# A Strassen product over two token blocks in the last layer-1 stage of an attention and maxout kernel

## The chip, the cores and the metric

The kernel runs on one core of one Trainium2 chip. The metric is the device time of one execution, in microseconds (us). TensorE does the matmuls, VectorE, ScalarE and GpSimd the elementwise work, and SyncE issues the transfers. In the profile these engines are called PE (PEld is its weight load), DVE, ACT, POOL and SP.

## The reference, cut to what matters

There are 8 batches, 8 heads, 576 positions of 64 numbers. The attention output of every token is the sum of two attentions: one over keys and values averaged four by four, repeated four times, and one over the local window of seven positions. Then every token's 512 numbers go through a maxout layer and an output layer:

```
h = np.maximum(np.maximum(x @ w1, x @ w2), x @ w3)    # x 4608 x 512, w 512 x 768
return (h @ w_out).astype(np.float32)                 # w_out 768 x 512
```

## The kernel before

Tokens are cut into blocks of 512. Block j (0 to 7) holds the first 512 tokens of batch j, and block 8 the last 64 tokens of each of the eight batches ("the tail block"). B is 8, so blocks B-1 and B are the last two.

For each block the attention is computed in two halves of four heads (`scores`, `pooled_scores`, `values`, `pooled_values`; n = 2j and 2j+1). The local window runs on VectorE, ScalarE and GpSimd: products `prod` and a reduction for the scores, then seven products per head into `pv` and a reduction over them into `x`. `transposes` turns `x` by TensorE, adds the pooled attention (`od`, `odtail`), and splits the result into a rounded part `xhi` and a remainder `xlo`. The weights are split in the same way into `whi` and `wlo` and stay in SBUF. A product of two split matrices is made of three matmuls: high by high, low by high, high by low.

`mlp_in(j)` is layer 1. For each of six groups of 128 hidden units (ft) and each of the three weight matrices (i) it does 4 chunks of 128 inputs times 3 matmuls, 12 in all, on 512 tokens, into one PSUM bank; the maximum over i is taken by VectorE, and the result is split into `hh`. One block takes 6 x 3 x 12 = 216 matmuls. `mlp_out(j)` is layer 2: 4 groups of 18 matmuls, a copy by ScalarE and a store.

All work is first recorded (`Recorder.add`) with a priority, and then `place` orders it: it goes through time with a cost for each operation, gives each engine the ready operation with the smallest start, priority and number, picks an engine where several may do an operation (`tt` allows VectorE and GpSimd), and hands out the buffers of each tag in the order of recording. The result is a fixed order on each engine. In that plan an operation of VectorE with two SBUF sources and any operation of GpSimd exclude one another (`port`). All instructions are issued in `emit`, so that the trace names line 390 for nearly all of them; tiles tell them apart. PSUM has four banks `pm`, three `pa` and one `pq`.

The main loop records `mlp_in(j)`, `mlp_out(j)`, then `turn(j + 1)` (the transposes of the next block) and `block(j + 2)` (the attention two blocks on). The high and low parts of x have one buffer each, so the parts of one block are made when layer 1 of the block before has ended.

Of the kernel before, what the change touches and what calls it, by code (L numbers as in the profile page):

```python
# [41 lines left out]
SETS = (5, 4, 3, 2, 5, 4, 5, 5)  # L42
STAGE = ("hh0", "hh1", "hh2", "hh3", "hh4", "hh5", "wo3", "wo4", "wo5", "hh3", "hh4", "hh5", "pv", "pv", "pv", "pv", "hh5", "pv")
STAGE_OUT = ("hh5", "hh4", "hh5", "hh4", "pv", "pv")
WO_ORDER = (2, 3, 4, 5, 0, 1)
F64_LO = float(np.array(0x38000000, np.uint32).view(np.float32))
F64_HI = float(np.array(0x47EFFFFF, np.uint32).view(np.float32))
# [40 lines left out]
class Recorder:  # L88
# [264 lines left out]
    def emit(self):  # L353
        out = self.place()
        store, words = {}, {}
        for tag, (bufs, infos) in self.tags.items():
            words[tag] = max(i["words"] for i in infos)

        def home(space, tag, i, kind):
            slot = (space, tag, i, kind)  # L360
            if slot not in store:
                name = f"{tag}_{i}"
                store[slot] = self.pools[space].tile([128, words[space, tag]], kind, tag=name, name=name + ("r" if kind == F32R else ""))
            return store[slot]

        def real(a):
            info = self.of.get(a.tensor.name) if is_ap(a) else None
            if info is None:
                return a
            (space, tag), width = info["tag"], words[info["tag"]]  # L370
            kind = F32R if info["dtype"] == F32R else F32
            base = home(space, tag, info["slot"], kind)
            dims = [list(d) for d in a.ap]
            p0, f0 = divmod(a.offset, dims[0][0])
            if a.dtype == BF16:
                base, width = base.bitcast(BF16), 2 * width
            dims[0][0] = width
            r = bass.AP(tensor=base.tensor, offset=base.offset + p0 * width + f0, ap=dims)
            return r if a.dtype in (kind, BF16) else r.bitcast(a.dtype)

        self.pools["SB"].tile([128, 8], F32, tag="pad", name="pad")
        for space, tag in self.tags:
            if tag.startswith(("whi", "wlo", "hh", "wo", "xhi", "xlo")) and tag != "hqk":
# [18 lines left out]
def local_global_attention_maxout_kernel(ctx: ExitStack, tc: tile.TileContext, q, k, v, w1, w2, w3, w_out, ident_d, mask_d, band_d, out):  # L402
# [285 lines left out]
    def values(n):  # L688
        j, h0 = n // 2, HH * (n % 2)
        st = state[n]  # L690
        p = st["p"]
        blk = state["blk", j]
        if j < B:
            hv = new([P, HH, 2 * D], tag="hv", name=f"hv_{n}")
            vd = st["vd"] = new([P, HH, D], tag="vd", bufs=2, name=f"vd_{n}")
        for g in range(HH):
            h = h0 + g
            if g % 2 == 0:
                x = blk["x"][h // 2] = new([P, FAC, 2, D], tag="x", bufs=XBUFS, name=f"x_{j}_{h // 2}")
# [186 lines left out]
    def mlp_out(j):  # L886
        h, wo = state["blk", j]["h"], state["wo"]
        for f in range(FAC):
# [10 lines left out]
                dst = dram(out, (FAC * P + f) * DM, [[S * DM, B], [FAC * DM, TAIL], [1, DM]])  # L899
            sp.dma_start(dst, y)  # L900

    def attention(n):
        j = n // 2
        if n % 2 == 0:
# [76 lines left out]


# [24 lines left out]
```

## Time and profile before

| what | value |
|---|---|
| time, median of 3 runs | 794.75 us (793.41 to 794.94) |
| time of the profiled execution | 794.03 us |
| its span in the trace | 792.3 us |
| TensorE busy | 751.6 us, 95% |
| VectorE busy | 623.9 us, 79% |
| ScalarE busy | 416.9 us, 53% |
| GpSimd busy | 311.4 us, 39% |

The span runs from the first to the last instruction of the trace; the time of the execution is 1.7 us longer. A matmul's recorded length is longer than the distance to the next one, since matmuls overlap in the array, so the price of one is read from a run of many.

### The profile page before, as it was taken

The numbers are of one execution on the slowest core, as the hardware profiler recorded it, in microseconds if no ns is written. First come the engines' busy times: TensorE is split into PE (matmuls) and PEld (weight loads), VectorE is DVE, ScalarE is ACT, GpSimd is POOL, SyncE is SP. The second block draws the span as 40 slices with busy tenths as digits, with TensorE's granted clock in tenths as the row PEclk, the third lists the DMA queues.
The fourth block names the chain that finished last, engine by engine and source line by source line (L and its number), as shares of the span: only waits on it lengthen the run. The fifth ranks groups of instructions, "written<-read, shape, count | busy, mean of one in ns | idle before, by whom it ended". The sixth has DMA issues, their size and how long they took to land. (4 is left out here: it accounts for less than half of the span.)

```text
span 792.3 us, 12159 instructions
## 1 busy us (share of the span) xinstructions
PE 751.6 (95%) x3992; PEld 593.9 (75%) x3992; DVE 623.9 (79%) x910; ACT 416.9 (53%) x1437; POOL 311.4 (39%) x555
## 2 busy tenths in 40 slices
PE   3889999999999999999999999899999999999997
PEld 2667777778787778677777887678777878888885
DVE  3889997998998999999999999899989765231220
ACT  2766676635755846577285545656583543121111
POOL 0000200225749738597584646657272423000000
PEclk9655999999999999999999999999999999999999
DMA  7985234315334334344254333433341211001002
GB/s 166 234 278 155 63 107 121 120 41 172 106 103 159 111 89 127 104 151 135 70 158 121 111 90 105 142 96 118 89 154 48 84 40 47 1 14 40 1 1 53
DMA packets 74293, 81.77 MB, mean 103 GB/s; under 512 B 29656, under 2 KB 54550, under 8 KB 74230
## 3 DMA queue, kind: packets, MB, share of 16 engines
q1 hardware_dynamic: 74230, 81.00, 34.3%
q8 instruction: 31, 0.51, 0.3%
q14 instruction: 32, 0.26, 0.1%
HBM read 71.54 MB, written 9.44 MB: 102 GB/s over the span
## 5 line engine op out<-in xcount | busy, mean ns | idle before, releaser
L390 PE MATMUL pm<-xhi_0r,wlo_0r 128*128 128x512 f32 x648 | 256.5, 396 | 0.3 <-DVE wlo_0r L390 0.3
L390 PE MATMUL pm<-xhi_0r,whi_0r 128*128 128x512 f32 x648 | 256.7, 396 | 0.0
L390 PE MATMUL pm<-xlo_0r,whi_0r 128*128 128x512 f32 x648 | 255.6, 395 | 0.0
L390 POOL TENSOR_TENSOR pv<-v,s 128x256 f32<-128x256 f32 x262 | 155.4, 698 | 83.8 <-DVE s L390 69.9
L390 PE MATMUL pm<-wo_0r,hh_0r 128*128 128x512 f32 x648 | 156.2, 394 | 1.3 <-DVE hh_0r L390 0.8
L390 PEld LDWEIGHTS pm<-xhi_0r,wlo_0r 128*128 128x128 f32 x648 | 122.5, 189 | 26.1 <-DVE wlo_0r L390 0.7
L390 PEld LDWEIGHTS pm<-xhi_0r,whi_0r 128*128 128x128 f32 x648 | 122.5, 189 | 25.8 <-issue 1.0
L390 PEld LDWEIGHTS pm<-xlo_0r,whi_0r 128*128 128x128 f32 x648 | 122.4, 189 | 25.5 <-issue 1.1
L390 ACT ACTIVATE pv<-v,s 128x64 f32<-128x64 f32 x520 | 136.4, 412 | 9.3 <-DMA v<-in_v_dram 4.8
L390 PEld LDWEIGHTS pm<-wo_0r,hh_0r 128*128 128x128 f32 x648 | 120.0, 188 | 27.6 <-DVE hh_0r L390 1.4
L390 DVE TENSOR_TENSOR prod<-k,pq 128x1792 f32<-128x1792 f32 x56 | 112.8, 2015 | 8.4 <-DMA k<-in_k_dram 5.5
L390 DVE TENSOR_REDUCE pq<-prod 128x28 f32<-128x1792 f32 x56 | 113.2, 2022 | 2.2 <-ACT pq L390 1.3
L390 DVE TENSOR_REDUCE x<-pv 128x256 f32<-128x1792 f32 x48 | 96.0, 2012 | 7.4 <-ACT pv L390 4.4
L390 ACT CAST hh_0r<-pm 128x512 fp32r<-128x512 f32 x54 | 31.8, 588 | 95.2 <-DVE pm L390 95.2
L390 DVE TENSOR_TENSOR t<-pm,t 128x512 f32<-128x512 f32 x54 | 37.0, 685 | 54.6 <-PE pm L390 54.1
L390 POOL TENSOR_TENSOR th<-traw 128x128 f32<-128x128 f32 x38 | 18.2, 480 | 128.8 <-DVE vs L390 74.2
L390 ACT COPY pq<-q 128x256 f32<-128x256 f32 x56 | 21.5, 384 | 67.1 <-DVE pq L390 37.6
L390 DVE TENSOR_TENSOR pm<-pm,t 128x512 f32<-128x512 f32 x54 | 37.4, 693 | 22.3 <-PE pm L390 21.9
L390 ACT COPY y<-pm 128x512 f32<-128x512 f32 x41 | 23.9, 590 | 49.9 <-PE pm L390 39.6
L390 ACT COPY t<-pm 128x512 f32<-128x512 f32 x54 | 31.8, 589 | 32.6 <-PE pm L390 32.4
L390 DVE TENSOR_TENSOR hh_0r<-pm,hh_0r 128x512 fp32r<-128x512 f32 x54 | 36.9, 684 | 9.8 <-ACT hh_0r L390 9.4
L390 POOL TENSOR_TENSOR hqk<-k 128x128 f32<-128x128 f32 x48 | 22.2, 464 | 29.2 <-DMA k<-in_k_dram 28.6
(160 smaller groups left out, 891.8 us busy)
## 6 DMA issues: line engine op xcount, KB each, us to landing
k<-in_k_dram SPq DMA_DIRECT2D x55, 320.0 KB
v<-in_v_dram SPq DMA_DIRECT2D x55, 320.0 KB
out_dram<-y SPq DMA_DIRECT2D x36, 256.0 KB
q<-in_q_dram SPq DMA_DIRECT2D x56, 128.0 KB
hh<-in_moe_w_dram SPq DMA_DIRECT2D x10, 512.0 KB
pv<-in_moe_w_dram SPq DMA_DIRECT2D x5, 512.0 KB
traw<-in_q_dram SPq DMA_DIRECT2D x16, 128.0 KB
v<-in_v_dram SPq DMA_DIRECT2D x16, 128.0 KB
```

The source lines that it names most:

```text
L390: getattr(self.engines[o.eng], method)(*map(real, args), **{k: real(x) for k, x in kw.items()})
```

## The change

Layer 1 of blocks 7 and 8 is no longer done block by block. For a pair of hidden groups (fa, fb) and one weight matrix (a step; there are nine) the product is a 2 by 2 block matrix product: the weights are cut by hidden group (fa, fb) and by input half (chunks 0 and 1, chunks 2 and 3), the tokens by block (7, 8) and by input half. Strassen's form (Winograd's variant) does it with 7 block products in place of 8. A block product is 2 chunks x 3 matmuls = 6 matmuls, so a step has 42 instead of 48. The four sums of weights are made per step by `combos` and split by `parts`; the sums of tokens are made once by `pair_operands`. The results are put together by additions behind the matmuls in `joint_in`. Layer 2 of both blocks follows. For the second half of the tail block's attention (n = 17) the `v` tiles of its last two heads take buffers of `k`, and VectorE may take the `pv` products too. The rest of the diff gives a buffer a new tile each time that its type changes.

```diff
-            vv = new([P, HW], tag="v", bufs=2, name=f"v_{n}_{g}")
+            vv = new([P, HW], tag="k" if n > 2 * B and g > 1 else "v", bufs=2, name=f"v_{n}_{g}")
...
-                rec.add({"ACT": muls, "POOL": [("tensor_tensor", (), kw)]})
+                one = [("tensor_tensor", (), kw)]
+                rec.spare = 0.0 if n > 2 * B else rec.spare
+                rec.add({"ACT": muls, "POOL": one, "DVE": one} if n > 2 * B else {"ACT": muls, "POOL": one})
...
+    def split(pair, src):
+        act.copy(pair[0], src)
+        tt(pair[1], src, pair[0].bitcast(F32), ALU.subtract)
+
+    def pair_operands():
...
+        state["sums"] = {0: combos(0)}
+        state["parts"] = {0: parts(0, state["sums"][0])}
+        prod, qkT, pvs = room("prod", 1, 3), room("qkT", 2, 1, wide) + room("qkT", 2, 1, wide), room("pv", 2, 3) + room("pv", 2, 3)
+        b22 = [tuple(room("k", 2) + room("hqk", 2)), tuple(room("k", 2) + room("pd"))]
...
+        for c in range(NCC):
...
+            for f in range(FAC):
+                pe.transpose(ps[:, f], x[:, f], ident)
...
+            dve.tensor_tensor(out=xc.rearrange("p (f r) -> p f r", f=FAC), in0=ps, in1=od, op=ALU.add)
+            if c < 2:
+                f = new([P, FAC * P], tag="od", bufs=2, name=f"t1_{c}")
+                f1.append(f)
+                tt(f, xc, blk["hi"][c].bitcast(F32), ALU.subtract)
+                tt(f, f, blk["lo"][c].bitcast(F32), ALU.subtract)
+                split(t1[c], f)
+        state["sums"][1] = combos(1)
+        state["parts"][1] = parts(1, state["sums"][1])
+        state["sums"][2] = combos(2)
+        rec.prio = -150.0
+        for c in range(2):
+            f, d, y = f1[c], xs[c], xs[c + 2]
+            tt(f, y, f, ALU.subtract)
+            split(t2[c], f)
+            tt(d, y, d, ALU.subtract)
+            split(t3[c], d)
+            split(b22[c], y)
...
+            tt(f, blk["hi"][c + 2].bitcast(F32), f, ALU.subtract)
+            tt(f, f, blk["lo"][c + 2].bitcast(F32), ALU.add)
+            split(t4[c], f)
...
+    def combos(step):
+        engines = ("DVE", "POOL") if step < 2 else ("POOL",)
...
+            f = [new([P, 2, 2 * P], tag=tag, bufs=bufs, name=f"f{x}_{step}") for x, (tag, bufs) in enumerate(homes)]
+        for x, ft in ((0, fa), (1, fb)):
+            flat = [w[ft][:, i].rearrange("p c t -> p (c t)").bitcast(F32) for w in (whi, wlo)]
+            tt(f[x].rearrange("p a t -> p (a t)"), *flat, ALU.add, engines)
+        (a11, a12), (a21, a22), (s1, s2), (s3, s4) = [(t[:, 0], t[:, 1]) for t in f]
+        tt(s1, a21, a22, ALU.add, engines)
+        tt(s2, s1, a11, ALU.subtract, engines)
+        tt(s3, a11, a21, ALU.subtract, engines)
+        tt(s4, a12, s2, ALU.subtract, engines)
...
+    def joint_in(xt):
...
+        def first(step):
...
+            product(ps, plain[:2], xt[1], True)
+            act.copy(p1, ps)
+            product(ps, plain[2:], xt[2], False)
+            if i == 0:
...
+                act.copy(low[ft], ps)
+            else:
+                dve.tensor_tensor(out=low[ft] if i == 1 else ps, in0=ps, in1=low[ft], op=ALU.max)
...
+        def second(step, t):
...
+            product(pd, w[1], xt[5], True)
+            act.copy(p5, pd)
...
+        for step in range(4):
+            early[step] = first(step)
+        for step in range(2):
+            early[step] += second(step, early[step][1])
+        for step in range(9):
...
+            if 0 < step < 8:
+                f = state["sums"].get(step + 1) or combos(step + 1)
+                state["parts"][step + 1] = parts(step + 1, f)
+            p1, t = early[step][:2] if step in early else first(step)
+            pd, w, p5 = early[step][2:] if step < 2 else second(step, t)
...
+            p6 = new([P, 4 * P], tag="x", bufs=XBUFS, name=f"p6_{step}")
+            product(pb, w[2], xt[6], True)
+            act.copy(p6, pb)
+            product(pb, w[3], xt[7], False)
+            dve.tensor_tensor(out=p5, in0=pb, in1=p5, op=ALU.add)
+            tt(p6, p1, p6, ALU.add)
+            product(pd, w[4], xt[3], False)
+            product(pb, w[7], xt[4], False)
...
+            tt(out[2], p5, p1, ALU.add)
+            dve.tensor_tensor(out=out[0], in0=pd, in1=p6, op=ALU.add)
+            dve.tensor_tensor(out=out[1], in0=pb, in1=p1, op=ALU.add)
+            if i > 0:
+                for r, src, engines in zip(run, out, (("DVE",), ("DVE",), ("DVE", "POOL"))):
+                    tt(r if i == 1 else src, src, r, ALU.max, engines)
...
-    for j in range(B + 1):
+    for j in range(B - 1):
         with at(-100.0):
             mlp_in(j)
             mlp_out(j)
-        if j < B:
-            turn(j + 1)
-        if j < B - 1:
-            block(j + 2)
+        turn(j + 1)
+        block(j + 2)
+    with at(100.0 * 2 * (B + 1)):
+        xt = pair_operands()
+    with at(-100.0):
+        joint_in(xt)
+        mlp_out(B - 1)
+        mlp_out(B)
```

`parts(step, f)`, not shown, splits the four sums of a step: in odd steps two casts and two subtractions of 128 x 512, in even steps four casts, three subtractions of 128 x 256 and two of 128 x 128. `finish`, not shown, is the cast and the subtraction that split a finished hidden group. `product` issues the 6 matmuls.

## Rows read from the trace of the kernel before

**Rows 1.** The page, its parts 1 and 2: busy time of each engine in the whole span, and the granted TensorE clock in forty equal slices (a digit is tenths of full speed).

```profile
PE 751.6 (95%) x3992; PEld 593.9 (75%) x3992; DVE 623.9 (79%) x910; ACT 416.9 (53%) x1437; POOL 311.4 (39%) x555
...
PEclk9655999999999999999999999999999999999999
```

**Rows 2.** The busy time of each engine in stretches of the second half (columns: stretch, then busy us and count for PE, weight load, VectorE, ScalarE, GpSimd; then granted clock, DMA share, GB/s).

```profile
620.00:640.00 20.00, 18.16 (x86) 14.72 (x86) 15.39 (x18) 7.52 (x21) 7.23 (x9) 1.00 0.16 48
640.00:657.70 17.70, 17.70 (x81) 14.45 (x80) 10.20 (x14) 10.09 (x34) 7.41 (x13) 1.00 0.28 87
657.70:704.50 46.80, 46.80 (x209) 38.67 (x208) 17.38 (x22) 10.32 (x22) 3.87 (x7) 1.00 0.01 5
704.50:786.60 82.10, 82.08 (x364) 67.65 (x362) 15.52 (x23) 12.23 (x21) 0.00 (x0) 1.00 0.08 23
```

**Rows 3.** The chain that ended last, from 637 us to the end (columns: start us, length us, what).

```profile
638.93 18.37 PE pm L390 x80
...
657.74 46.75 PE pm L390 x206
...
704.93 81.67 PE pm L390 x360
...
786.66 0.59 ACT y L390
```

**Rows 4.** VectorE in order of time near the end of the kernel, around layer 2 of the last full block and after it.

```profile
702.88 2.05 DVE L390 TENSOR_TENSOR xlo_0r<-pa,xhi_0r 128x512 fp32r<-128x512 f32 x3 [0.31 <-ACT xhi_0r L390]
...
726.85 0.69 DVE L390 TENSOR_TENSOR t<-pm,t 128x512 f32<-128x512 f32 x1 [18.64 <-PE pm L390]
729.50 0.70 DVE L390 TENSOR_TENSOR pm<-pm,t 128x512 f32<-128x512 f32 x1 [1.96 <-PE pm L390]
730.85 0.69 DVE L390 TENSOR_TENSOR hh_0r<-pm,hh_0r 128x512 fp32r<-128x512 f32 x1 [0.65 <-ACT hh_0r L390]
```

**Rows 5.** Groups of one operation and shape, GpSimd over the whole span (columns: instruction, count, busy us, mean ns of one, idle before).

```profile
L390 POOL TENSOR_TENSOR pv<-pv 128x512 f32<-128x512 f32 x8 | 10.0, 1252 | 0.6
...
L390 POOL TENSOR_TENSOR qd<-hqk 128x256 f32<-128x256 f32 x12 | 8.9, 740 | 7.0 <-PE pa L390 6.9
...
L390 POOL TENSOR_TENSOR th<-pd 128x128 f32<-128x128 f32 x1 | 0.5, 454 | 15.3 <-DMA pd<-in_k_dram 15.3
```

**Rows 6.** The same kind of groups for VectorE between 40 and 200 us.

```profile
L390 DVE TENSOR_TENSOR wlo_0r<-hqk,whi_0r 128x512 fp32r<-128x512 f32 x16 | 11.0, 686 | 1.6 <-ACT whi_0r L390 1.5
...
L390 DVE TENSOR_TENSOR t<-pm,t 128x512 f32<-128x512 f32 x8 | 5.5, 685 | 1.0 <-PE pm L390 1.0
...
L390 DVE TENSOR_TENSOR vd<-hv 128x256 f32<-128x256 f32 x3 | 1.3, 418 | 0.0
```

**Rows 7.** The same kind of groups for ScalarE between 40 and 200 us: casts that read SBUF, casts that read PSUM, and quarters of a local-window product.

```profile
L390 ACT CAST whi_0r<-hqk 128x512 fp32r<-128x512 f32 x17 | 10.6, 626 | 4.2 <-DVE hqk L390 4.2
...
L390 ACT CAST hh_0r<-pm 128x512 fp32r<-128x512 f32 x7 | 4.1, 588 | 5.6 <-DVE pm L390 5.6
...
L390 ACT ACTIVATE pv<-v,s 128x64 f32<-128x64 f32 x16 | 4.0, 409 | 0.0
```

**Rows 8.** VectorE in order of time from 80 us, where two-source SBUF operations follow one another.

```profile
80.63 0.68 DVE L390 TENSOR_TENSOR wlo_0r<-hqk,whi_0r 128x512 fp32r<-128x512 f32 x1
81.23 1.29 DVE L390 TENSOR_TENSOR xlo_0r<-t,xhi_0r 128x512 fp32r<-128x512 f32 x2
...
83.90 0.68 DVE L390 TENSOR_TENSOR q<-whi 128x256 f32<-128x256 f32 x1
```

**Rows 9.** GpSimd in order of time, the stretch of Rows 8.

```profile
80.62 2.54 POOL L390 TENSOR_TENSOR th<-pt 128x128 f32<-128x128 f32 x1 [22.21 <-PE pa L390]
83.24 0.58 POOL L390 TENSOR_TENSOR vs<-th 128x64 f32<-128x64 f32 x1
```

**Rows 10.** VectorE in order of time, the last attention (the chunk of tail tokens) and what follows (columns: start us, length us, instruction, and in brackets the idle time before it and what ended it).

```profile
642.40 2.02 DVE L390 TENSOR_REDUCE pq<-prod 128x28 f32<-128x1792 f32 x1
...
646.28 0.27 DVE L390 TENSOR_TENSOR s<-pq,z 128x112 f32<-128x112 f32 x1
650.54 2.02 DVE L390 TENSOR_REDUCE x<-pv 128x256 f32<-128x1792 f32 x1 [3.99 <-ACT pv L390]
...
654.00 2.02 DVE L390 TENSOR_REDUCE x<-pv 128x256 f32<-128x1792 f32 x1
...
658.61 2.02 DVE L390 TENSOR_REDUCE x<-pv 128x256 f32<-128x1792 f32 x1
...
661.98 2.02 DVE L390 TENSOR_REDUCE x<-pv 128x256 f32<-128x1792 f32 x1 [0.21 <-POOL pv L390]
```

**Rows 11.** GpSimd in order of time, the stretch of Rows 10.

```profile
646.63 5.28 POOL L390 TENSOR_TENSOR pv<-v,s 128x256 f32<-128x256 f32 x9 [18.78 <-DVE s L390]
655.58 3.01 POOL L390 TENSOR_TENSOR pv<-v,s 128x256 f32<-128x256 f32 x5 [3.66 <-DMA v<-in_v_dram]
658.96 2.98 POOL L390 TENSOR_TENSOR pv<-v,s 128x256 f32<-128x256 f32 x5 [0.38 <-DMA v<-in_v_dram]
```

**Rows 12.** TensorE in order of time: idle gaps before single groups of matmuls.

```profile
601.18 1.09 PE L390 MATMUL pa<-ident,x 128*128 128x128 f32 x8 [1.23 <-ACT odtail L390]
...
637.00 1.25 PE L390 MATMUL pa<-ident,x 128*128 128x128 f32 x8 [1.84 <-DVE xlo_0r L390]
```

More of the change, by code (lines that the diff above doesn't have):

```diff
@@ L44 @@
 STAGE_OUT = ("hh5", "hh4", "hh5", "hh4", "pv", "pv")
+ALIGNED = ("prod", "pv", "hqk", "hv", "pd", "pt", "qkT", "k", "v", "q", "qd", "kd", "traw", "vd", "tq", "th")
+H_LAST = ("whi0", "wlo0", "whi2", "wlo2", "whi3", "wlo3")
 WO_ORDER = (2, 3, 4, 5, 0, 1)
@@ L357, in emit, with home @@
             words[tag] = max(i["words"] for i in infos)
-        def home(space, tag, i, kind):
-            slot = (space, tag, i, kind)
+            last, turns = {}, {}
+            for i in infos:
+                kind = i["dtype"] == F32R
+                if last.get(i["slot"]) != kind:
+                    last[i["slot"]] = kind
+                    turns[i["slot"], kind] = turns.get((i["slot"], kind), -1) + 1
+                i["turn"] = turns[i["slot"], kind]
+        def home(space, tag, i, kind, turn=0):
+            slot = (space, tag, i, kind, turn)
             if slot not in store:
                 name = f"{tag}_{i}"
-                store[slot] = self.pools[space].tile([128, words[space, tag]], kind, tag=name, name=name + ("r" if kind == F32R else ""))
+                store[slot] = self.pools[space].tile([128, words[space, tag]], kind, tag=name, name=name + ("r" if kind == F32R else "") + (f"t{turn}" if turn else ""))
             return store[slot]
@@ L371, in real @@
             kind = F32R if info["dtype"] == F32R else F32
-            base = home(space, tag, info["slot"], kind)
+            base = home(space, tag, info["slot"], kind, info["turn"])
             dims = [list(d) for d in a.ap]
@@ L382, in emit @@
         for space, tag in self.tags:
-            if tag.startswith(("whi", "wlo", "hh", "wo", "xhi", "xlo")) and tag != "hqk":
+            if tag.startswith(("whi", "wlo", "hh", "wo", "xhi", "xlo")) or tag in ALIGNED:
                 for i in range(self.tags[space, tag][0]):
@@ new lines, in combos @@
+    def combos(step):
+        engines = ("DVE", "POOL") if step < 2 else ("POOL",)
+        fa, fb, i = 2 * (step // 3), 2 * (step // 3) + 1, step % 3
+        if step == 1:
+            f = [new([P, 2, 2, 2 * P], tag=tag, name=f"f_{tag}_{step}") for tag in ("hh0", "hh1")]
+            f = [t[:, x] for t in f for x in range(2)]
+        else:
+            homes = [("hv", 1), ("pd", 1), ("qkT", 2), ("qkT", 2)] if step == 0 else [("x", XBUFS)] * 4
+            f = [new([P, 2, 2 * P], tag=tag, bufs=bufs, name=f"f{x}_{step}") for x, (tag, bufs) in enumerate(homes)]
[7 more added lines that the diff above has]
+        tt(s4, a12, s2, ALU.subtract, engines)
+        return f
@@ new lines, in parts @@
+    def parts(step, f):
+        fb, i = 2 * (step // 3) + 1, step % 3
+        (a11, a12), (a21, a22), (s1, s2), (s3, s4) = [(t[:, 0], t[:, 1]) for t in f]
+        s = {}
+        if step % 2 == 0:
+            homes = [("q", 2), ("q", 2), ("vd", 2), ("vd", 2), ("qd", 1), ("kd", 1), ("traw", 1)]
+            t = [new([P, 2 * P], F32R, tag=tag, bufs=bufs, name=f"sum{x}_{step}") for x, (tag, bufs) in enumerate(homes)]
+            halfs = [[u[:, c * P : c * P + P] for c in range(2)] for u in t]
+            halfs.append([new([P, P], F32R, tag=tag, name=f"sum_{tag}_{step}") for tag in ("tq", "th")])
+            for x, m, src in ((0, 2, s2), (1, 1, s1), (2, 3, s3), (3, 4, s4)):
+                s[m] = list(zip(*halfs[2 * x : 2 * x + 2]))
+                if m != 4:
+                    split(t[2 * x : 2 * x + 2], src)
+                    continue
+                act.copy(t[6], src)
+                for c, (hi, lo) in enumerate(s[m]):
+                    tt(lo, src[:, c * P : c * P + P], hi.bitcast(F32), ALU.subtract)
+        else:
+            tags = ("hh2", "hh3") if step < 4 else ("whi1", "wlo1")
+            hi, lo = [new([P, 2, 4 * P], F32R, tag=tag, name=f"s_{tag}_{step}") for tag in tags]
+            for x in range(2):
+                split((hi[:, x], lo[:, x]), f[2 + x].rearrange("p a t -> p (a t)"))
+            for m in range(1, 5):
+                x, o = (m - 1) // 2, (m - 1) % 2 * 2 * P
+                s[m] = [tuple(t[:, x, o + c * P : o + c * P + P] for t in (hi, lo)) for c in range(2)]
+        s[7] = [(whi[fb][:, i, c], wlo[fb][:, i, c]) for c in range(2, NCC)]
+        return s
```

66 lines of the change are left out of this document (added).

## The prediction

> **What bounds the kernel now.** I read the page first. TensorE is busy for 95% of the span, and its granted clock is full (2.4 GHz) from the fourth of forty slices on [rows 1]. So a matmul less is worth its price at that clock, if TensorE stays the engine that ends last where it is taken out. The stretches of the second half show whether it does. Up to 640 us VectorE is at 15.4 of 20 us beside TensorE's 18.2. From 640 us TensorE has no gap, while VectorE falls to 17.4 of 46.8 us and then 15.5 of 82.1, ScalarE to 10 and 12, GpSimd to 3.9 and none [rows 2]. The chain that ended last says the same: from 638.9 us it is matmuls alone, up to one copy and the last store [rows 3]. This is the stage that the change rewrites. It has room on three engines and none on TensorE.
>
> A matmul's price comes from the chain: 206 in 46.75 us and 360 in 81.67 us, both 0.2269 us [rows 3]. The first run has mostly groups of 12 into one bank, the second many of 18; the price does not move, so I give groups of 6 the same.
>
> **What is removed.** Nine steps with 6 matmuls less are 54 matmuls: 54 x 0.2269 = 12.25 us. Layer 1 of both blocks goes from 432 to 378 matmuls, 98.0 to 85.8 us. Layer 2, the transposes and the stores stay. Gone too are the four casts and four subtractions that split the tail block's x (2.05 us for three of them [rows 4]); they lay beside matmuls, so I give nothing for them.
>
> **What is added beside the matmuls, per step.** TensorE needs 42 x 0.2269 = 9.53 us for a step; each other engine has to stay below that.
> - GpSimd, from the third step on: two sums of 128 x 512 and four of 128 x 256. At 1.252 and 0.740 us [rows 5] that is 5.46 us.
> - VectorE with a PSUM source: three additions, two maxima (three in two steps of three), one split: 6 x 0.685 = 4.1 us [rows 6].
> - VectorE with two SBUF sources: p6, the third sum, its maximum and its split in part, 3 x 0.685 = 2.06 us; and the splits of the weight sums, 2 x 0.685 in odd steps, at most 5 x 0.418 in even ones [rows 6], about 1.6 us. Together 3.7 us, so VectorE has 7.8 us.
> - ScalarE: three casts or copies from PSUM, some 1.7 more for the plain product and the finished groups, at 0.588, and two to four of the weight sums at no more than 0.626 [rows 7]: about 4.5 us.
>
> Each is below 9.53 us alone. What speaks against adding them up separately is one place in the trace. A GpSimd addition of 128 x 128, 0.454 us when alone [rows 5], started at 80.62 and took 2.54 us, just while VectorE ran three two-source operations from 80.63 to 82.52 [rows 8, 9]. After it a VectorE addition of 128 x 256 took 0.68 us, beside a mean of 0.418 [rows 6, 8]. So in this kernel the two kinds queue behind one another, and I add them: 5.46 + 3.7 = 9.2 us, 97% of a step.
>
> The Trainium skill, "SBUF — State Buffer", section "Who interferes with whom", states this as a rule: a VectorE instruction with two SBUF inputs and a GpSimd instruction that reads SBUF exclude each other for their whole length, and the loser waits. By that rule a step has 9.2 us on the common port, without it 7.8 us at most on one engine. The trace agrees with the rule, by the 2.54 us.
>
> **What is moved: the start of the joint stage.** Layer 1 of block 7 started by itself at 657.7 us and needed nothing of the tail block before 702.9 us, when its x was split [rows 3, 4]. Now that x is needed within some 12 us. In the trace the last reduction into x ends at 664.0 (661.98 + 2.02) [rows 10]. It is late for a reason that the change touches: GpSimd waited 3.66 us for v, and VectorE idled 3.99 us for the products [rows 10, 11]. The scores are done at 646.55 [rows 10]. From there are left 28 products and four reductions of 2.02 us. GpSimd makes a product in 5.28 / 9 = 0.59 us [rows 11], ScalarE in four parts of 4.0 / 16 us, 1.0 in all [rows 7], VectorE, an estimate by the 128 x 256 addition, in 0.42 [rows 6]. In T us GpSimd and ScalarE make 2.7 T, VectorE (T - 8.1) / 0.42; 28 products need T = 9.3. With v loaded earlier and the last reduction behind the last product I take 658.5 as the end of x. The bounds are 656 (all engines full) and 664 (nothing gained).
>
> From there the common port has work in a row. Sixteen two-source operations of 128 x 512 for the token sums, at a spacing of 0.60 us (from 80.63 to 81.23 [rows 8]), are 9.6 us. Before them stand the last four transposes (half of the 1.25 us of eight [rows 12]), an addition of 0.69 and the signals between, about 1.7 us, so they end at 669.8. The weight sums of the second step, if nothing of them got done before, are 4 x 0.60 + 4 x 0.42 = 4.1 us: 673.9. Those of the third on GpSimd, 5.5 us, and their split and the first additions behind, about 3 us: 682.5.
>
> TensorE meanwhile has four `first` products (48 matmuls), one `second`, and the rest of step 0: 78 matmuls or 17.7 us, up to 675.4. So the operands come just in time, with a margin of one or two us. A group that continues in a bank after a copy or an addition has to wait for it; where no other group covers that I expect gaps like those of 1.2 and 1.8 us that stand before transposes today [rows 12]. I take 2.0 us for the start, between 0 and 7.5 (2.0, and the 5.5 by which x may come at 664).
>
> Later the weight sums run behind one another. Those of the third step are ready 24.8 us after the start (682.5 - 657.7), those of the ninth six periods on: 24.8 + 6 x 9.2 = 80.0. TensorE wants them after all other work before, 348 matmuls or 79.0 us. That is 1.0 us late; it is nothing with a period of 9.0 and grows by 6 us for each us of period.
>
> At the end the last hidden groups are finished while layer 2 of block 7 has five of six groups to multiply first: 60 matmuls in four banks, 13.6 us, over a chain of four operations of about 0.7 us. I cost it at nothing; without that cover it would be about 3.5 us.
>
> **Sum.** - 12.25 + 2.0 + 1.0 = - 9.25 us: the span goes from 792.3 to 783.05 and the profiled execution from 794.03 to 784.8. The median of the runs is 0.7 us above the profiled one, so 794.75 - 9.25 = 785.5 us.
>
> **Rivals.**
> - *No gap at all.* VectorE and GpSimd have over 60% free from 657.7 us [rows 2], and some weight sums can be made before, while GpSimd waits (18.8 us idle before 646.63 [rows 11]). Then the whole 12.25 us come through: 782.5 us. Against it: 97% on the common port.
> - *Operands late, still faster.* x at 664 costs 5.5 us more, or a period of 10 costs 24.8 + 60 - 79 = 5.8 us in place of 1.0: 790 to 791 us.
> - *The common port paces the joint stage: slower than before.* VectorE executes in order, so a two-source operation that waits for GpSimd holds the PSUM additions behind it, and TensorE waits for their banks. VectorE has 7.8 us per step, 6.3 of its operations have two sources, and a GpSimd operation is 0.91 us on average. If each waits for half a one, the period is 7.8 + 6.3 x 0.455 = 10.7, and the delay 24.8 + 6 x 10.7 - 79 = 10 us, which with the 2.0 of the start eats the gain: that is the point from which it decides. At three quarters the period is 12.1, the delay 18.4 us and the time 802.9 us. For it: the 2.54 us. Against it: the recorded order keeps the two kinds apart in its plan, and six GpSimd operations fill only 5.5 of 9.5 us.
> - *The change does less than it says.* Shorter groups might raise a matmul's price. 12 and 18 cost the same [rows 3], so I give this no chance of its own.
>
> **How the numbers follow.** Forecast with gaps of 1 to 6 us, 783.5 to 788.5: 0.58. No gap, 782 to 783.5: 0.15. Operands late, 788.5 to 793: 0.16. Slower than before by the port: 0.11. The range 782 to 791.5 holds the first two and most of the third, about 8 in 10. About 0.2% (1.6 us) is what a measurement can tell from no change. Faster than 793.2: the first three, less a little at the edge: 0.85; same 0.05; slower 0.10.
>
> **What would show it.** 3938 matmuls in place of 3992. From 640 us to the end TensorE's idle time should be 2 to 5 us, most of it before 690, with VectorE near 80% and GpSimd near 60% between 690 and 740. The last x should end near 658.5. In steps three to nine the distance from step to step should be near 9.5 us; a distance above 10.7 with TensorE waiting for weight sums is the slower rival. I am wrong if TensorE has no such gaps, if a matmul costs other than 0.227 us there, or if the work before 640 us got longer because weight sums were put into it.

## The result

The change makes the kernel slower: 800.95 us (median of 4 runs, 800.25 to 803.15) against 794.08 us (793.29 to 794.94) for the kernel before, run beside it. The ratio is 1.0091, with a 95% interval from 1.0067 to 1.0115. The forecast was 785.5 us. The profiled execution of the changed kernel took 800.25 us and its span is 798.5 us, 6.2 us more than before.

The first part of the page after, against [rows 1]:

```profile
span 798.5 us, 12240 instructions
...
PE 745.4 (93%) x3938; PEld 582.6 (73%) x3938; DVE 698.6 (87%) x1023; ACT 436.7 (55%) x1477; POOL 354.7 (44%) x593
...
PEclk9655999999999999999999999999999999999999
```

The 54 matmuls are gone, and TensorE is busy for 6.2 us less in a span that is 6.2 us longer: TensorE waits. Where it waits, the stretches of the second half show (columns as in [rows 2]):

```profile
640.00:660.00 20.00, 15.98 (x72) 12.66 (x71) 19.63 (x28) 8.42 (x28) 5.86 (x8) 1.00 0.17 57
660.00:680.00 20.00, 17.28 (x67) 12.62 (x65) 20.00 (x28) 10.40 (x23) 8.97 (x9) 0.92 0.04 14
680.00:700.00 20.00, 16.84 (x68) 12.36 (x68) 19.16 (x31) 6.16 (x14) 9.13 (x9) 1.00 0.00 1
700.00:720.00 20.00, 18.79 (x80) 14.43 (x80) 18.40 (x27) 7.62 (x16) 14.69 (x14) 1.00 0.00 0
720.00:740.00 20.00, 18.11 (x79) 14.28 (x78) 17.57 (x26) 8.04 (x17) 11.74 (x11) 1.00 0.00 1
740.00:760.00 20.00, 20.00 (x89) 15.95 (x88) 15.40 (x25) 5.23 (x11) 5.32 (x5) 1.00 0.00 1
760.00:798.50 38.50, 32.75 (x145) 26.77 (x143) 4.61 (x8) 6.49 (x11) 0.00 (x0) 0.97 0.19 55
```

TensorE had no gap here in [rows 2]; now it does 67 to 80 matmuls per 20 us up to 740 us, where a full stretch holds 20 / 0.2269 = 88. VectorE is at 96% or more from 640 to 700 us and at 88% or more up to 740.

Two places have to be told apart. The first is the start, up to about 675 us. VectorE works on the tail block's x, in one row without a gap, while ScalarE and GpSimd wait for it:

```profile
648.83 6.42 DVE L399 TENSOR_TENSOR pv<-v,s 128x256 f32<-128x256 f32 x9
655.07 3.94 DVE L399 TENSOR_REDUCE x<-pv 128x256 f32<-128x1792 f32 x2
658.90 5.33 DVE L399 TENSOR_TENSOR pv<-k,s 128x256 f32<-128x256 f32 x5
664.07 3.91 DVE L399 TENSOR_REDUCE x<-pv 128x256 f32<-128x1792 f32 x2
...
657.11 2.09 ACT L399 ACTIVATE pv<-k,s 128x64 f32<-128x64 f32 x8 [5.23 <-DVE x L399]
...
657.15 3.62 POOL L399 TENSOR_TENSOR pv<-k,s 128x256 f32<-128x256 f32 x5 [4.38 <-DVE x L399]
```

VectorE makes 14 of the 28 products and all four reductions. The products go into `pv`, which has two buffers, and a buffer comes free when its reduction has ended; so ScalarE idles 5.23 us and GpSimd 4.38 us until the first reduction is over. The last reduction ends at 667.98, where it ended at 664.0 before [rows 10] and was forecast for 658.5. TensorE waits for x in front of both sets of transposes, and after the longer wait it runs on at the lower clock:

```profile
659.06 0.66 PE L399 MATMUL pa<-ident,x 128*128 128x128 f32 x4 [3.12 <-DVE x L399]
660.04 0.63 PE L399 MATMUL pm<-xhi_0r,wlo_0r 128*128 128x512 f32 x1
660.46 0.63 PE L399 MATMUL pm<-xlo_0r,whi_0r 128*128 128x512 f32 x1
...
668.03 0.66 PE L399 MATMUL pa<-ident,x 128*128 128x128 f32 x4 [1.65 <-DVE x L399]
```

From 660.04 to 663.4 the matmuls start 0.427 us apart (the granted clock of the stretch 660 to 680 us is 0.92: part of it at 1.2 GHz), then 0.227 again.

The second place is the joint stage from 680 to 740 us. VectorE, GpSimd and TensorE around 690 us:

```profile
688.17 0.68 DVE L399 TENSOR_TENSOR hh_0t<-pa,hh_0t 128x512 f32<-128x512 f32 x1
689.24 0.29 DVE L399 TENSOR_TENSOR tq_0r<-x,traw_0r 128x128 fp32r<-128x128 f32 x1 [0.39 <-ACT traw_0r L399]
689.45 1.78 DVE L399 TENSOR_TENSOR od<-hh_0t 128x512 f32<-128x512 f32 x1
691.15 1.36 DVE L399 TENSOR_TENSOR th_0r<-x,traw_0r 128x128 fp32r<-128x128 f32 x1
692.43 0.68 DVE L399 TENSOR_TENSOR hh_0t<-pa,hh_0t 128x512 f32<-128x512 f32 x1
...
689.26 3.10 POOL L399 TENSOR_TENSOR x<-whi_0r,wlo_0r 128x512 f32<-128x512 f32 x2
...
693.17 0.50 PE L399 MATMUL pa<-hv_0r,whi_0r 128*128 128x512 f32 x1 [1.56 <-DVE hh_0t L399]
```

A 128 x 128 subtraction takes 1.36 us beside GpSimd's weight sums, and its equal just before them 0.29. Behind it stands an addition that reads PSUM (`hh_0t<-pa,hh_0t`) and has nothing to do with GpSimd; TensorE waits 1.56 us for it. Some groups of the stretch 684 to 744 us (columns: count, busy us, mean ns of one, idle before):

```profile
L399 DVE TENSOR_TENSOR th_0r<-x,traw_0r 128x128 fp32r<-128x128 f32 x3 | 4.1, 1369 | 0.0
L399 DVE TENSOR_TENSOR wlo_0r<-hh_0t,wlo_0r 128x512 fp32r<-128x512 f32 x2 | 2.4, 1223 | 0.0
L399 POOL TENSOR_TENSOR x<-whi_0r,wlo_0r 128x512 f32<-128x512 f32 x12 | 17.7, 1488 | 12.7 <-DVE t L399 7.8 <-DVE pa L399 4.9
L399 POOL TENSOR_TENSOR x<-x,x 128x256 f32<-128x256 f32 x16 | 16.0, 1008 | 1.3 <-DVE th_0r L399 0.6 <-DVE q_1r L399 0.5
```

Both sides are longer than in [rows 5, 6]: GpSimd's sums by 0.24 and 0.27 us, VectorE's two-source operations by up to 1.1. Not every operation pays: of the 41 two-source operations that VectorE does in this stretch (128 x 128 to 128 x 512), 24 have their own length, and 17 run over it, by 0.67 us on the average and 11.4 us together.

The waits of TensorE that the profile lists from 680 to 745 us add up to 6.4 us; 3.3 of them end with an operation of VectorE and 3.1 with one of ScalarE. The longest, 1.89 us at 736.52, ends with a copy in a row of ScalarE whose first operation had waited 2.95 us for VectorE.

### The profile page after: what moved, and what is told of

Read it like the earlier page. It is cut to its first block, busy times and chain, and to the rows that moved or that the text cites. A ratio compares the mean times of both kernels' runs of the same rounds, so it can differ in the third digit from the quotient of the medians.

```text
span 798.5 us, 12240 instructions
## 1 busy us (share of the span) xinstructions
PE 745.4 (93%) x3938; PEld 582.6 (73%) x3938; DVE 698.6 (87%) x1023; ACT 436.7 (55%) x1477; POOL 354.7 (44%) x593
## 4 chain that ended last, share of the span: by engine, by line
PE 39%; DVE 30%; issue 8%; POOL 8%; ACT 6%; DMA 6%; SPq 1%; ACTq 0%; POOLq 0%; DVEq 0%
PE pm L399 32%; PE pa L399 7%; POOL pv L399 6%; DVE prod L399 5%; DVE pq L399 5%; DVE hqk L399 3%; DVE x L399 2%; DMA traw<-in_v_dram 2%; DVE xlo_0r L399 1%; DVE pm L399 1%; SPq L399 1%; DVE t L399 1%; DVE pa L399 1%; DVE wlo_0r L399 1%; DVE hh_0r L399 1%
## 5 line engine op out<-in xcount | busy, mean ns | idle before, releaser
L399 PE MATMUL pm<-xhi_0r,whi_0r 128*128 128x512 f32 x540 | 215.4, 400 | 0.9 <-ACT y L399 0.9
L399 PE MATMUL pm<-xhi_0r,wlo_0r 128*128 128x512 f32 x540 | 215.2, 399 | 0.3 <-DVE wlo_0r L399 0.3
L399 PE MATMUL pm<-xlo_0r,whi_0r 128*128 128x512 f32 x540 | 214.1, 397 | 0.0
L399 POOL TENSOR_TENSOR pv<-v,s 128x256 f32<-128x256 f32 x246 | 146.5, 700 | 69.3 <-DVE s L399 63.0
L399 ACT ACTIVATE pv<-v,s 128x64 f32<-128x64 f32 x492 | 129.4, 411 | 10.1 <-DMA v<-in_v_dram 5.0
L399 PE MATMUL pm<-wo_0r,hh_0r 128*128 128x512 f32 x528 | 129.5, 396 | 2.2 <-DVE hh_0r L399 1.7
L399 PEld LDWEIGHTS pm<-xhi_0r,whi_0r 128*128 128x128 f32 x540 | 102.7, 190 | 24.0 <-ACT y L399 1.9
L399 PEld LDWEIGHTS pm<-xhi_0r,wlo_0r 128*128 128x128 f32 x540 | 102.7, 190 | 22.0 <-DVE wlo_0r L399 0.7
L399 PEld LDWEIGHTS pm<-xlo_0r,whi_0r 128*128 128x128 f32 x540 | 102.4, 190 | 21.3 <-issue 1.1
L399 PEld LDWEIGHTS pm<-wo_0r,hh_0r 128*128 128x128 f32 x528 | 97.5, 188 | 24.0 <-DVE hh_0r L399 2.7
L399 POOL TENSOR_TENSOR th<-traw 128x128 f32<-128x128 f32 x38 | 18.6, 488 | 131.8 <-DVE vs L399 75.8
```

## The experiments

The first theory after the result had these two causes: **S**, the weight sums on GpSimd hold VectorE up for the rest of the stage; and **P**, the products that VectorE makes for the tail make x late. The rival to both was that VectorE simply has too much to do.

The "loss" below is worked out from the starts of TensorE's matmuls in each trace: the sum of what each start-to-start distance has above 0.2269 us (0.112 for a transpose). Each trace is one execution. From 655 us to the end of the matmuls the loss is 0.0 before, and:

| kernel | time, us | ratio to before | lost 655 to 680 | lost after 680 |
|---|---|---|---|---|
| the change | 800.95 | 1.0091 | 8.9 | 9.7 |
| no products on VectorE | 798.15 | 1.0051 | 4.8 | 11.1 |
| no weight sums | 790.5 | 0.9965 | 7.2 | 1.3 |
| x early | 794.4 | 1.0006 | 5.6 | 6.9 |
| x early and no weight sums | 785.38 | 0.9889 | 1.2 | 1.2 |

**No products on VectorE (a_no_dve).**

```diff
-                rec.spare = 0.0 if n > 2 * B else rec.spare
-                rec.add({"ACT": muls, "POOL": one, "DVE": one} if n > 2 * B else {"ACT": muls, "POOL": one})
+                rec.add({"ACT": muls, "POOL": one})
```

> The changed kernel, but the local-window products of the tail block's second half go to ScalarE and GpSimd alone again; the v tiles in k buffers stay. Theory P (VectorE's share in these products made x late: they cost 0.66 to 1.7 us each where about 0.4 was planned, and the last x came at 668.0 us): the last x comes near 660 to 664 and the time falls by 4 to 7 us, to 794 to 797 us. Theory S (the weight sums on GpSimd and VectorE's two-source operations block one another, in the joint steps above all): the time falls by less than 2 us, and the delay after the last x stays. Theory O (TensorE's fixed order and its half clock after a gap): both gaps before the tail's transposes shrink only if x comes earlier, so under 4 us.

798.15 us, ratio 1.0051 (1.0031 to 1.0072): 3.2 us less by the ratios, between what P (4 to 7) and S (under 2) gave. The first three reductions into x end 2.3, 0.5 and 3.9 us earlier than with the change, and neither set of transposes waits any more; but the last x, at 668.4, is not earlier:

```profile
649.01 3.07 ACT L399 ACTIVATE pv<-v,s 128x64 f32<-128x64 f32 x12 [0.18 <-DMA k<-in_v_dram]
...
657.72 1.10 ACT L399 COPY hh_0t<-pm 128x512 f32<-128x512 f32 x2
658.71 0.62 ACT L399 CAST prod_0r<-od 128x512 fp32r<-128x512 f32 x1
...
663.70 1.12 ACT L399 ACTIVATE pv<-k,s 128x64 f32<-128x64 f32 x4
...
654.92 5.83 POOL L399 TENSOR_TENSOR pv<-k,s 128x256 f32<-128x256 f32 x8
...
666.40 2.01 DVE L399 TENSOR_REDUCE x<-pv 128x256 f32<-128x1792 f32 x1
```

GpSimd's products end at 660.7, ScalarE's only at 664.8: between its 48 quarter products ScalarE does eight copies and casts, six of them of the joint stage and two of layer 2 of the block before. And the last reduction starts 1.6 us after the last product, behind seven operations of the joint stage on VectorE (662.12 to 666.4). So here the last x is late because the new stage's own work shares the engines that make x. With the change it is late because VectorE has 14 products and four reductions to do in one row, from 648.83 to 667.98. Theory P holds for the first three parts of x; for the last part, taking VectorE's products away only lets the new stage's work into their place.

**No weight sums (a_no_sums).**

```diff
+        if step > 1:
+            for t in f:
+                gps.memset(t.rearrange("p a t -> p (a t)"), 0.0)
+            return f
```

Four writes of zeros, which read nothing, stand in place of the six sums of a step.

> The changed kernel, but the six weight sums on GpSimd are left out from the third step on: four writes of zeros stand in their place, so those steps multiply by wrong weights, and the splits behind them stay. Theory S: VectorE's two-source operations lose their waits, 6.4 us in the joint steps and some 4 us beside the tail's products, and the time falls by 7 to 10 us, to 791 to 794 us, with VectorE's two-source additions of 128x512 at 0.60 to 0.69 us everywhere. Theory P alone: the products stay near 0.66 us, x comes at 664 or later and the time stays within 3 us of 801.

790.5 us, ratio 0.9965 (0.9951 to 0.9979), 10.0 us less by the ratios, a little more than expected. VectorE's operations have their own length again, and the profile lists no wait of TensorE from 680 to 745 us. A group of 684 to 744 us (its mean is 840 ns with the sums there), and then two stretches:

```profile
L399 DVE TENSOR_TENSOR hh_0t<-hh_0t 128x512 f32<-128x512 f32 x4 | 2.8, 689 | 0.1
```

```profile
680.00:700.00 20.00, 20.00 (x89) 15.99 (x88) 19.86 (x35) 10.29 (x22) 10.78 (x18) 1.00 0.00 1
700.00:720.00 20.00, 20.00 (x88) 15.95 (x87) 13.78 (x23) 6.29 (x14) 5.27 (x10) 1.00 0.00 1
```

Theory S holds for the stage behind 680 us. In 680 to 700 us VectorE is at 99% and TensorE still full, so VectorE's own load was not the limit.

**x early (a_early_x), and both (a_no_sums_early_x).**

```diff
-            for o in range(NO):
+            for o in range(3 if n > 2 * B else NO):
...
+            if n > 2 * B:
+                dve.tensor_reduce(out=xo, in_=pv[..., :3], axis=AX.X, op=ALU.add)
+                continue
```

In the second half of the tail block only three of the seven products of a head are made and added up.

> The change, with only three of the seven products of the last local window in the tail's last attention made and added (the other four are left out of x), so that x is ready earlier; the weight sums stay on GpSimd. Theory T (two causes that add): with the sums taken out, the early x was worth 5.1 us (790.5 to 785.4), so here 800.9 - 5.1 = 795 to 797 us. Rival (the causes overlap: while the weight sums pace the stage, an earlier x only moves the wait to a later step): 799 to 801 us, and TensorE loses in 680 to 740 us what it no longer loses before 675.

> The kernel of a_no_sums, and for the second half of the tail block only three of the seven local-window products of a head are made and added up, so that its x is ready some 5 us earlier (and wrong). Theory T (two causes and no third: the weight sums, and x of the tail block that comes late): TensorE's lost time after 640 us falls from 9.6 us to 3 to 5 us and the time from 790.5 to 784 to 787 us, the forecast of the prediction. Rival O (TensorE's fixed order and the operations behind x set the loss, not x itself): the time stays above 788.5 us.

794.4 us, ratio 1.0006 (0.9992 to 1.0021), and 785.38 us, ratio 0.9889 (0.9871 to 0.9907). The last reductions of the two:

```profile
657.01 1.79 DVE L399 TENSOR_REDUCE x<-pv 128x256 f32<-128x768 f32 x2
```

```profile
L399 DVE TENSOR_REDUCE x<-pv x4: 920/928/931, 650.8 to 655.5; 128x256 f32<-128x768 f32 x4
```

x is complete at 658.8 and 656.4. By the ratios, times 794.1 us, an early x is worth 6.7 us with the sums there and 6.0 without them, the sums 10.0 and 9.3. The two gains add, and with both out the kernel is at 785.4 us with 2.4 us lost: there is no third cause of size, and the rival, that the wait only moves on, fell in both. The forecast of 785.5 us is met more closely than the interval (0.18% to either side, 1.4 us) can tell, by a kernel that leaves work out.

The two causes do not split by place. Leaving out the sums saves 1.7 us before 680 us and 8.4 behind it when x is late, 4.4 and 5.7 when x is early; and an early x alone lowers the loss behind 680 us from 9.7 to 6.9. Sums of the joint stage also meet VectorE while it makes x: three products beside a sum of 128 x 512 take 1.50 to 1.55 us each with the change, where one alone takes 0.49.

**The disputed cost by itself (b_probe).** The kernel before, with 36 products and eight additions behind its last block: twelve VectorE products of 128 x 256 into every seventh element and twelve into neighbouring ones, six on GpSimd, two additions, and six VectorE products beside six GpSimd additions of 128 x 512.

```diff
+        for o in range(6):
+            rec.add({"DVE": mul(o, 1, sums[0][:, :256], each)})
+            gps.tensor_tensor(out=sums[1], in0=sums[0], in1=y, op=ALU.add)
```

> The kernel before with 36 operations behind its last block that nothing waits for: a product of 128x256 with two SBUF sources on VectorE, six times in each of four forms (result spread with a stride of 7 numbers or dense; second source one number per 64 or dense), then six on GpSimd alone, then six on VectorE beside six additions of 128x512 on GpSimd. If the spread result makes the product slow: 0.66 us spread and 0.42 dense, whatever the second source. If the repeated second source does: 0.66 with it and 0.42 without. If only GpSimd beside it does: 0.42 in all four alone. Beside GpSimd, if the two exclude each other: single products of 1.2 us or more and additions of more than 1.25 us, their sum at least 6 x 1.2 plus 6 x 0.5 us of wall time; if they share: both at their lengths alone. The time of this kernel is longer by the added operations and is not compared.

One run, 813.57 us. The groups at its end:

```profile
L390 DVE TENSOR_TENSOR pv<-y 128x256 f32<-128x256 f32 x12 | 5.7, 622 | 14.9 <-ACT y L390 14.9
L390 DVE TENSOR_TENSOR x<-y 128x256 f32<-128x256 f32 x12 | 5.1, 424 | 0.4
L390 DVE TENSOR_TENSOR pv<-x,y 128x256 f32<-128x256 f32 x6 | 8.6, 1563 | 4.6 <-POOL x L390 4.6
L390 POOL TENSOR_TENSOR x<-x,y 128x512 f32<-128x512 f32 x6 | 8.3, 1389 | 0.5
```

A product with its result spread over every seventh element is recorded for 0.62 us, a dense one for 0.42. The spacing of the starts is 0.46 us in both, but the dense ones wrote the same buffer in turn, so the probe's spacing does not tell the two apart. The changed kernel's does: spread products alone follow one another after 0.49 us (653.11 to 655.07), and behind a dense operation of this size the next starts after 0.33 (669.05 and 669.99).

Beside GpSimd, six products take 8.6 us: each waits until the running addition of GpSimd has ended. VectorE's product gets 2.5 times as long, GpSimd's addition a tenth longer (1.39 us against the 1.252 of [rows 5]). One point came out otherwise than expected for two operations that exclude each other: a product and an addition together take 1.47 us from start to start, less than 0.46 and 1.25 us after one another. So they overlap in part.

**Fewer two-source operations (a_fold).** p1 is added when PSUM is read, so that two copies on ScalarE and two two-source additions per step fall away; two block products of a step move behind these additions.

```diff
-            act.copy(p5, pd)
+            dve.tensor_tensor(out=p5, in0=pd, in1=p1, op=ALU.add)
...
-            act.copy(p6, pb)
+            dve.tensor_tensor(out=p6, in0=pb, in1=p1, op=ALU.add)
...
-            dve.tensor_tensor(out=p5, in0=pb, in1=p5, op=ALU.add)
-            tt(p6, p1, p6, ALU.add)
...
-            tt(out[2], p5, p1, ALU.add)
+            dve.tensor_tensor(out=out[2], in0=pb, in1=p5, op=ALU.add)
```

> The changed kernel, but the first product is added while the PSUM banks are read (two additions with one PSUM source in place of two ScalarE copies and two additions with two SBUF sources per step). Theory S: 18 fewer two-source operations of which half waited about 0.6 to 1.1 us, so 3 to 6 us less, 795 to 798 us. Against it: TensorE now waits for VectorE where it waited for ScalarE, which is idle half of the time; then the time stays at 800 to 803 us.

799.14 us, ratio 1.0071 (1.0048 to 1.0095), a miss: 1.6 us where 3 to 6 were expected. In its trace 31 two-source operations are left between 684 and 744 us, of which eight still run over their length, by 6.1 us together, and the loss behind 680 us falls from 9.7 to 8.1 us, while the loss before it rises from 8.9 to 10.3. Why the gain is no larger was not tested; the rival of the expectation, that TensorE now waits for VectorE where it waited for ScalarE, stays open.

**Towards a better version.** Three edits on top of it. First, from the third step on the splits of the sums, and one finished group, on GpSimd alone (c_fold_pool); then that without VectorE products (c_nodve_fold_pool); then that with the last two parts of the tail's x left in PSUM, so that the token sums have a PSUM source (c_nodve_fold_pool_psumy).

```diff
+        eng = ("DVE", "POOL") if step < 2 else ("POOL",)
...
-                    split(t[2 * x : 2 * x + 2], src)
+                    split(t[2 * x : 2 * x + 2], src, eng)
...
-            xc = new([P, FAC * P], tag=tag, bufs=bufs, name=f"xs_{B}_{c}")
+            xc = new([P, FAC * P], tag=tag, bufs=bufs, name=f"xs_{B}_{c}") if c < 2 else ps.rearrange("p f r -> p (f r)")
...
-            tt(f, y, f, ALU.subtract)
+            dve.tensor_tensor(out=f, in0=y, in1=f, op=ALU.subtract)
```

> The kernel of a_fold, and from the third step on also the splits of the weight sums and of one finished group go to GpSimd alone, so that VectorE has only maxima left with two SBUF sources in a step (0.4 us of them). All sums stay. Theory S (VectorE loses time by waiting for GpSimd, one whole GpSimd operation for each two-source one): VectorE's waits in the joint steps vanish and the time falls by 3 to 6 us against the changed kernel, to 795 to 798 us. Rival G (GpSimd's own length sets the pace): GpSimd has 5.5 + 2.1 us of 9.5 per step and gets no pause, so the time is 800 us or more.

> The kernel of c_fold_pool with the tail's products on ScalarE and GpSimd alone, as in a_no_dve. If the two edits act in different places their gains add: 2 to 3 us below c_fold_pool. If the sums of the second and third step, which GpSimd makes beside these products, only move behind them, the time is that of c_fold_pool.

> The kernel of c_nodve_fold_pool, and the last two parts of the tail's x stay in PSUM, so that six of the sixteen operations behind x have one SBUF source and GpSimd can work beside them. Theory S: these six wait for nothing, and the chain behind x, 18 us in the changed kernel, is shorter by 2 to 4 us; the time falls by 1 to 3 us. If VectorE's own length sets that chain, it stays within 1 us of c_nodve_fold_pool.

797.16 us, ratio 1.0035 (1.0018 to 1.0052); 792.88 us, 0.9974 (0.9959 to 0.9989); 788.2 us, 0.9924 (0.9901 to 0.9947). The first came as expected; the other two gained more than expected (4.8 and 4.0 us by the ratios). Behind 680 us TensorE loses 4.6, 2.5 and 1.5 us in the three, after 8.1 in a_fold: the less VectorE has that can meet GpSimd, the less TensorE waits, although all sums stay. The last version beats both kernels, by 0.76% the one before. Its joint stage, and its one large gap (the traced execution, 790.95 us, was the slowest of its four):

```profile
680.00:700.00 20.00, 19.70 (x86) 15.87 (x86) 16.26 (x25) 5.59 (x12) 18.28 (x21) 1.00 0.00 1
700.00:720.00 20.00, 19.90 (x87) 15.93 (x87) 12.75 (x18) 5.53 (x11) 18.56 (x22) 1.00 0.00 1
```

```profile
672.35 0.80 PE L399 MATMUL pm<-k_0r,traw_0r 128*128 128x512 f32 x1 [3.31 <-DVE hh_0t L399]
672.94 0.63 PE L399 MATMUL pm<-k_0r,tq_0r 128*128 128x512 f32 x1
```

GpSimd is now at 92%, more than VectorE, and TensorE almost full: what matters is that VectorE's queue no longer stops, not that work is spread evenly. The gap that is left ends with an addition on VectorE at 671.62; in front of it stand four two-source operations that take up to 1.78 us, beside GpSimd's sums again.

**Is it TensorE's written order? (d_price, d_best_lag3, d_best_lag5).** The order is fixed by a plan that prices a VectorE product at 62 + 1.045 x 256 = 330 ns. d_price doubles that in the changed kernel; with it the plan gives VectorE no product at all, so this run is no test of the order alone. The other two take the 788.2 us version and tell the plan that the tail's transposes are free 2.4 and 4.4 us later, so that they stand later among the matmuls. The edits of d_price and d_best_lag3:

```diff
-            return 62.0 + 1.045 * n, big >= 2
+            return (62.0 + 1.045 * n) * (2.0 if kw.get("op") == ALU.mult and n == FAC * D and big >= 2 and method == "tensor_tensor" else 1.0), big >= 2
```

```diff
-                pe.transpose(ps[:, f], x[:, f], ident)
+                with at(rec.prio, 3000.0):
+                    pe.transpose(ps[:, f], x[:, f], ident)
```

> The change, with VectorE's products of the local windows priced at 0.66 us in the plan in place of 0.33, near what the trace shows; nothing else is edited, the engines and orders that follow from it are the planner's. Theory O (the order was written out from a price that was too low, so transposes that wait for x stand too early): 797 to 799 us, with the gaps before 672 us down from about 6 to 3 us. Rival (x is late because the joint stage's own work fills the engines that make it, whatever the plan believes): 800 to 802 us, the last reduction into x at 667 or later and the gaps as long as before.

> The version without VectorE products, with the folded additions, the splits on GpSimd and the last two parts of x kept in PSUM (788.2 us), in which the plan takes the tail's last transposes to be free 2.4 us later than before: they stand 13 and 9 matmuls later in TensorE's order, and nothing else is edited. Theory O (TensorE's fixed order puts transposes, and what hangs on them, in front of matmuls that are ready): the gap of 3.5 us at 668.65 and most of the 2.6 us at the lower clock behind it go, 783 to 786 us. Rival (the matmuls behind need the same x, so that the gap only moves): 787 to 789 us with a gap of 3 us or more between 668 and 680.

> The same version with the transposes taken to be free 4.4 us later: 22 and 15 matmuls later in TensorE's order. Theory O: 783 to 787 us, no gap above 1.5 us before 672 us; where the delay is longer than x needs, the time is that of the run with 2.4 us or up to 1 us more. Rival (the gap only moves): 787 to 790 us.

799.67 us, ratio 1.0081 (1.005 to 1.0113); 790.09 us, 0.9949 (0.9934 to 0.9963); 788.87 us, 0.9936 (0.9915 to 0.9958). None gains beyond its interval. In d_price the last x ends at 670.9. With the later transposes the gap of 3.31 us is smaller, and others stand behind it. Two lines of d_best_lag5:

```profile
672.76 0.50 PE L399 MATMUL pm<-k_0r,traw_0r 128*128 128x512 f32 x1 [0.99 <-DVE hh_0t L399]
677.17 0.80 PE L399 MATMUL pm<-k_1r,traw_0r 128*128 128x512 f32 x1 [1.64 <-ACT k_1r L399]
```

Between 670 and 680 us TensorE loses 5.5 us there. The first wait ends with an addition in VectorE's queue, the second with a cast of the tail's x. So the written order alone is not the cause: what stands behind hangs on the same x and the same queue. What would make x earlier without leaving products out stays open.

## Why the prediction was wrong

**Right:** what is removed. There are 3938 matmuls, and where the stage runs free (740 to 760 us) most stand 0.227 us apart, as in [rows 3]. One in six distances is 0.24 to 0.27 us, so that 42 matmuls take 9.7 us in place of 9.53. Over nine steps that is about 1.5 us (an estimate from this difference), which the sum had at nothing. The end of the stage cost nothing, as said: nothing is lost behind 745 us.

**The step that failed most: "That is 1.0 us late; it is nothing with a period of 9.0".** The term was 1.0 us and measured 9.3 to 10.0, by the kernels without the sums (5.7 to 8.4 of it as loss behind 680 us). The working added the GpSimd sums and the two-source operations to 9.2 us per step, 97% of 9.53, and took this as the period. The sum of the port's work is not what sets the pace. A two-source operation that meets GpSimd's row of sums takes up to 1.1 us longer (1.36 us for 128 x 128, 1.78 for 128 x 512), and the PSUM additions, which keep their own length, stand still behind it. By 42 matmuls of TensorE's order, counted back from the end of the stage, the last seven steps are 12.1, 12.8, 9.6, 9.6, 11.9, 9.7 and 9.7 us long, 10.8 on the average.

That is the third rival, and nearly its numbers: it gave 10.7 us and 10 us of delay. It was given 0.11. Its price of a meeting is not what was measured, though: it let every two-source operation wait 0.455 us, and the 11.4 us over 41 operations are 0.28 each. Its total came out near the measured one by some luck.

What was put against it was that the recorded order keeps the two kinds apart in its plan. That was no row of the trace, and the trace after shows it false: the `th` splits met a sum each of three times (mean 1369 ns). The 2.54 us of [rows 9], put for it, were read too simply: there GpSimd paid, and the three operations of VectorE beside it kept their length [rows 8]. Of the 93 two-source operations of this kind in the trace before (128 x 128 to 128 x 512), none ran over its length by more than 0.26 us (the 0.68 at 83.90). Which of the two pays in a row of meetings was not in the trace, and the probe that settles it was run only afterwards.

The rule of the Trainium skill ("SBUF — State Buffer", section "Who interferes with whom") was cited for the sum; it also says that the loser blocks. The probe agrees with that (1.56 us for a product of 0.62), but not with an exclusion for the whole length of both: a pair takes 1.47 us, less than 0.46 and 1.25. What the prediction's sum left out was to follow the loser's queue.

**The second step: "I take 2.0 us for the start, between 0 and 7.5".** 8.9 us were lost between 655 and 680 us. With the sums out it is 7.2, and an early x takes 6.0 of them away. Three parts of the step were wrong.
- The end of x: 658.5 forecast, 667.98 measured, outside the bounds of 656 to 664. The 9.3 us for 28 products let three engines work all the time and left VectorE about three products. VectorE made 14, in one queue with the four reductions: at 0.49 us each, with 7.7 us for the reductions, that is 14.6 us from 648.83 on. About 4.5 us more went to meetings with GpSimd, 3.1 of them with three sums of the joint stage. The wait for v did go, as forecast, but the waits for a buffer of `pv` took its place (5.23 and 4.38 us). "664 (nothing gained)" is no bound on the late side: without VectorE's products the joint stage's copies, casts and subtractions hold the last part back (a_no_dve). Moving a dependency earlier moved its competitors there too. The scores, too, are ready 1.8 us later, behind three operations of the joint stage on VectorE (645.37 to 647.43).
- The VectorE product: 0.42 us was the recorded length of an addition with a dense result. What counts in a queue is the distance to the next, 0.49 us for these products alone and 0.69 on the average of the first nine, which met GpSimd three times. With 0.49 the working gives 9.4 us in place of 9.3, so the price was no large part of the miss. The Trainium skill ("SBUF — State Buffer", section "Door 1: The DMA port swizzle") says that fp32 elements can be 4 apart for free and that more costs; here they are 7 apart, and the rows agree in the direction (0.49 against 0.33).
- The price of a gap: it was counted as its own length. The 3.12 us before the transposes also cost eight matmuls at 0.427 us, 1.6 us more.

**A reading:** [rows 1] has the clock at full speed from the fifth slice, not the fourth; nothing rests on it.

**The signs:** the last x, the step distance, and TensorE's lost time (18.6 us from 655 us in place of 2 to 5) are all off to the same side. VectorE is at 92% in 680 to 740 us, not 80; of that a part is waiting, since blocked time counts as busy: without the sums it is at 79% there.

## What to carry to other kernels

Where two engines exclude each other, do not stop at adding up their work and comparing the sum with the stage. List the operations that can meet the other engine, and ask what stands behind each in its queue and who waits for that. A price for one meeting has to come from a row of meetings, as in the probe, and it is paid by a part of the operations only: here by 17 of 41, at 0.67 us. Operations that are freely placed cost less here when they were all on one side of the exclusion (sums and splits on GpSimd, and on VectorE sources in PSUM), even though that engine then looked full. And when work is moved in front of a new dependency, the bound on the late side has to include the new stage's own work on the engines that make the operand, and the buffers that tie those engines together; "no later than before" is not one.

## What was not expected of the hardware

- A 128 x 256 fp32 product on VectorE whose result goes to every seventh element is recorded for 0.62 us and lets the next start after 0.49 (in the changed kernel); a dense operation of this size 0.42 and 0.33.
- In the probe, with both engines issuing back to back, the exclusion was not shared evenly: VectorE's product went from 0.62 to 1.56 us, GpSimd's addition from 1.25 to 1.39. In the changed kernel GpSimd's sums paid 0.24 and 0.27 us each, 7 us in all from 684 to 744 us.
- A wait of TensorE of about 3 us could leave it at 1.2 GHz: eight matmuls at 0.427 us after 3.12 us in the changed kernel, and in the 788.2 us version twelve after 3.31 us. It need not: after 3.22 us at 678.80 in c_nodve_fold_pool the clock stayed at 2.4 GHz and the matmuls at 0.23 us.
